# A fused attention and MLP kernel whose matrix products move to halves of TensorE's rows

## The chip, the core and the metric

The kernel runs on one core of a Trainium2 chip. Five engines take part, each with its own instruction queue: TensorE (PE) multiplies matrices, VectorE (DVE), ScalarE (ACT) and GpSimd (POOL) work on elements, and SyncE (SP) issues the transfers (DMA). A product on TensorE has a stationary operand, which a weight load (PEld) puts into the array, and a moving operand, whose columns stream past it. The contraction runs over the rows of the array, which are the 128 partitions of the on-chip memory. Products are summed up in PSUM, which has eight banks. The metric is the device time in microseconds (us), the median of several runs.

## The reference

The input x has 2048 rows of 640. It is normalized, goes through an attention with 32 heads of 20 and a sliding window of 256, and through an MLP of width 1536; the MLP's output gates the attention's.

```
xn = _layernorm(x, axis=-1)
qkv = (xn @ wqkv).reshape(B, S, 3, H, Dh)          # H = 32, Dh = 20
scores = einsum("bhqd,bhkd->bhqk", q, k) * Dh**-0.5
scores = where((i - j >= 0) & (i - j < 256), scores, -1e9)
o = einsum("bhqk,bhkd->bhqd", softmax(scores), v)
s = o.reshape(B, S, D) @ wo
r = maximum(xn @ w1 + b1, 0)
g = silu((r * r) @ w2 + b2)
return x + s * g
```

## The kernel before

The work has three stretches. The first normalizes and transposes x, makes all of V and the first group of Q and K. The middle runs the attention over 16 pairs of heads and 16 tiles of 128 queries, in `steps` = 16·16 + 12 steps, and fills the time on TensorE between its products with the dense products that are left: 32 groups of 15 products for Q and K (tile `qkps`, 512 columns), 48 groups of 15 for the MLP's first matrix (`hps`, 512 columns) and 64 groups of 18 for its second (`yps`, 320 columns). The last stretch multiplies by `wo` (`wops`) and gates.

A dense product is made of three fp32r products (a 4-byte type): each operand is split into a high part and a rest, and high·high, high·rest and rest·high are summed. Q and K for the scores are split into three bf16 parts each. Six pairs of parts lie one under the other, 6·20 = 120 rows (`KR`), so that one product sums them up. The parts are written to memory (`qk_stores`) and read back per pair of heads (`pair_loads`) into `qs` and `ks`.

One step of the middle does, in this order: two score products `sps` of the two heads (`scores`, L448), two products `stps` of the transposed scores of an earlier tile (`scores_t`, L492), the row maxima on DVE (`maxima`, L460), every fourth step the transposition of the maxima (L474) and their copy `mrow` (L478), exponentials on ACT (L499), masking on POOL (L500, L502), a share of the filler (`fill`), the split of the exponentials into two fp16 parts `ph` (ACT, L507) and `pl` (DVE, L513), evacuations of finished dense groups (`flush`), the rest of the filler, and every second step the products with V of two tiles (`values`, L527, 61 columns each, 24 in a full job of two tiles and two heads). What a dense group leaves in PSUM is taken out by `evac`: for Q and K two ACT copies (L780, L784), a DVE subtraction (L781) and a POOL subtraction (L785).

The order of all five queues is written out by hand (`manual_schedule`): what the code emits first stands first. `fill` draws as many products from the generator `filler` as its running total of `cost` allows. PSUM has three banks for dense groups (`pmm`), two for `sps`, two for `stps` and one for the products with V (`po`).

## Time and profile before

| what | us |
|---|---|
| runs | 916.62, 915.09, 917.11 (median 916.62) |
| span of the profiled execution, first to last instruction | 913.8 |
| PE busy | 893.6 (98%) |
| DVE busy | 759.1 (83%) |
| ACT busy | 668.6 (73%) |
| POOL busy | 544.9 (60%) |

The profiled execution's own time outside the span is not listed; its span is 2.8 us under the median of the runs. Matmuls are pipelined and their ends are modelled in the trace, so a busy share of 98% on PE does not yet say that no more would fit. The chain of work that ended last lists, in order of time, what the end of the program hung on; its stretches of like products give the time from one product to the next.

### The profile page before, as it was taken

The numbers are of one execution on the slowest core, as the hardware profiler recorded it, in microseconds if no ns is written. First come the engines' busy times: TensorE is split into PE (matmuls) and PEld (weight loads), VectorE is DVE, ScalarE is ACT, GpSimd is POOL, SyncE is SP. The second block draws the span as 40 slices with busy tenths as digits, with TensorE's granted clock in tenths as the row PEclk, the third lists the DMA queues.
The fourth block names the chain that finished last, engine by engine and source line by source line (L and its number), as shares of the span: only waits on it lengthen the run. The fifth ranks groups of instructions, "written<-read, shape, count | busy, mean of one in ns | idle before, by whom it ended". The sixth has DMA issues, their size and how long they took to land.

```text
span 913.8 us, 21792 instructions
## 1 busy us (share of the span) xinstructions
PE 893.6 (98%) x7632; PEld 746.9 (82%) x7632; DVE 759.1 (83%) x2031; ACT 668.6 (73%) x1282; POOL 544.9 (60%) x832
## 2 busy tenths in 40 slices
PE   8999999999999999999999999999999999999998
PEld 8999977776766678788788788778788788789998
DVE  7875478999899998998888999998988988975554
ACT  5454348898889896987886988976986977994321
POOL 6010017797789785886785876775775976772000
PEclk9999999999999999999999999999999999999999
DMA  6899786767777454244264245365174264156873
GB/s 240 279 394 350 219 266 201 233 209 237 250 237 237 142 180 131 89 155 132 67 203 152 69 123 153 103 224 152 51 262 136 75 211 145 27 158 222 286 272 117
DMA packets 130803, 168.79 MB, mean 185 GB/s; under 512 B 44100, under 2 KB 91268, under 8 KB 128132
## 3 DMA queue, kind: packets, MB, share of 16 engines
q1 hardware_dynamic: 130692, 167.39, 56.3%
q8 instruction: 60, 0.98, 0.4%
q14 instruction: 51, 0.42, 0.1%
HBM read 96.15 MB, written 70.91 MB: 183 GB/s over the span
## 4 chain that ended last, share of the span: by engine, by line
PE 73%; DVE 9%; ACT 8%; DMA 4%; issue 3%; POOL 2%; SPq 1%; ACTq 0%; DVEq 0%; POOLq 0%
PE yps L872 14%; PE hps L578 14%; PE wops L578 8%; PE sps L448 7%; PE qkps L578 7%; PE ops L527 7%; PE stps L492 6%; PE vps L230 5%; ACT p L499 3%; DVE junk L460 2%; PE qkps L200 2%; DVE pl L513 2%; ACT ph L507 1%; DMA v_d<-vt 1%; ACT relu L827 1%
## 5 line engine op out<-in xcount | busy, mean ns | idle before, releaser
L499 ACT ACTIVATE p<-stps,ebias 128x384 f32<-128x384 f32 (+2 forms) x512 | 258.7, 558 | 85.2 <-PE stps L492 72.9
L460 DVE CUSTOM_DVE_ANT_0 junk<-sps,mask 128x384 bf16<-128x384 f32 (+2 forms) x512 | 250.5, 525 | 47.3 <-PE sps L448 40.8
L513 DVE TENSOR_TENSOR pl<-p,ph 128x768 f16<-128x768 f32 (+2 forms) x256 | 251.3, 982 | 1.9 <-ACT ph L507 1.9
L500 POOL TENSOR_SCALAR_AFFINE_SELECT p<-p 128x256 f32<-128x256 f32 x256 | 166.9, 652 | 128.4 <-ACT p L499 112.0
L507 ACT ACTIVATE ph<-p 128x768 f16<-128x768 f32 (+2 forms) x256 | 204.6, 799 | 4.1 <-POOL p L502 3.0
L872 PE MATMUL yps<-w,hh 128*128 128x320 f32 x768 | 183.8, 320 | 0.0
L578 PE MATMUL hps<-xb,w 128*128 128x512 f32 x630 | 172.1, 410 | 0.0
L578 PEld LDWEIGHTS hps<-xb,w 128*128 128x128 f32 x630 | 115.3, 188 | 24.1
L872 PEld LDWEIGHTS yps<-w,hh 128*128 128x128 f32 x768 | 130.7, 188 | 5.0 <-issue 0.6
L448 PE MATMUL sps<-ks,qs 120*128 120x384 bf16 (+2 forms) x512 | 128.2, 319 | 4.5 <-DVE mt L460 4.4
L872 PE MATMUL yps<-w,hl 128*128 128x320 f32 x384 | 122.5, 319 | 0.0
L492 PE MATMUL stps<-qs,ks 122*128 122x384 bf16 (+2 forms) x512 | 120.8, 316 | 1.2 <-DMA qs<-mrow 1.0
L502 POOL TENSOR_SCALAR_AFFINE_SELECT p<-p 128x256 f32<-128x256 f32 x224 | 109.0, 487 | 0.0
L527 PEld LDWEIGHTS <-ph 128*128 128x128 f16 x1440 | 85.9, 97 | 25.6 <-issue 20.6
L527 PE MATMUL ops<-vp,ph 128*128 128x61 bf16 x1440 | 100.9, 192 | 0.0
L527 PE MATMUL ops<-vp,pl 128*128 128x61 bf16 x1440 | 99.7, 191 | 0.0
L831 POOL TENSOR_TENSOR hl<-sq,hh 128x256 fp32r<-128x256 f32 x96 | 77.5, 808 | 18.9 <-DVE sq L830 15.6
L527 PEld LDWEIGHTS <-pl 128*128 128x128 f16 x1440 | 87.7, 97 | 0.0
L872 PEld LDWEIGHTS yps<-w,hl 128*128 128x128 f32 x384 | 72.2, 188 | 1.5
L492 PEld LDWEIGHTS <-ks 122*128 122x128 bf16 x512 | 49.0, 98 | 29.5 <-issue 2.5
L230 PE MATMUL vps<-wv,xT 128*128 128x320 f32 x480 | 71.7, 308 | 0.2 <-DVE r L255 0.2
L230 PEld LDWEIGHTS vps<-wv,xT 128*128 128x128 f32 x480 | 70.5, 188 | 0.6 <-DVE r L255 0.5
(116 smaller groups left out, 1480.3 us busy)
## 6 DMA issues: line engine op xcount, KB each, us to landing
ks<-k_d SPq DMA_DIRECT2D x64, 240.0 KB
qs<-q_d SPq DMA_DIRECT2D x64, 240.0 KB
xb<-xs SPq DMA_DIRECT2D x12, 1280.0 KB
xs<-xT SPq DMA_DIRECT2D x8, 1280.0 KB
y<-ysb SPq DMA_DIRECT2D x32, 320.0 KB
q_d<-shm SPq DMA_DIRECT2D x38, 256.0 KB
v_d<-vt SPq DMA_DIRECT2D x8, 976.0 KB
vp<-v_d SPq DMA_DIRECT2D x16, 488.0 KB
```

Of the source, the lines that this page charges most:

```text
L230: nc.tensor.matmul(ps, xT[xp][b][:, c * BT + t * P: c * BT + (t + 1) * P], wv[wp][:, c, nh * HALF:(nh + 1) * HALF], start=first and m == 0 ...
L448: nc.tensor.matmul(ps[:, :nk], qs[i][0:KR, hh, q * P:(q + 1) * P], ks[i][0:KR, hh, k0 * P:k0 * P + nk], start=True, stop=True)
L460: nc.vector.tensor_tensor_reduce(out=junk[:, :nk], in0=r[hh][:, :nk], in1=mask[:, 3 * P - nk:], scale=1.0, scalar=-3.0e38, op0=ALU.add, op ...
L492: nc.tensor.matmul(ps[:, :n], ks[i][0:KR + 2, hh, kb * P:(kb + 1) * P], qs[i][0:KR + 2, hh, kb * P:kb * P + n], start=True, stop=True)
L499: nc.scalar.activation(p32[:, hh, :n], r[hh][:, :n], AF.Exp, scale=SCALE, bias=ebias)
L500: nc.gpsimd.affine_select(p32[:, :, 0:P], p32[:, :, 0:P], pattern=[[0, 2], [1, P]], compare_op=ALU.is_ge, fill=0.0, base=0, channel_multip ...
L502: nc.gpsimd.affine_select(p32[:, :, 2 * P:], p32[:, :, 2 * P:], pattern=[[0, 2], [-1, P]], compare_op=ALU.is_gt, fill=0.0, base=0, channel ...
L507: nc.scalar.activation(ph[:, :, :n], p32[:, :, :n], AF.Copy)
L513: nc.vector.tensor_sub(pl[:, :, :n], p32[:, :, :n], ph[:, :, :n])
L527: nc.tensor.matmul(ot[:, q % 4, hh, :], t[:, hh, (q - k) * P:(q - k + 1) * P], vp[:, k // 4, k % 4, hh, :], start=m == 1, stop=m == 2 * le ...
L578: nc.tensor.matmul(ps, a, b_, start=j == 0, stop=j == n - 1)
L872: nc.tensor.matmul(pss[nh], hs[fc][hp][:, tt * P:(tt + 1) * P], lin1(wt2, (wp * NFH + fc) * D + nh * HALF, HALF), start=fc == 0 and j == 0 ...
```

## The change

**Halves.** In the middle every product is emitted for 64 of TensorE's 128 rows (`HP`). A dense product and a product with V become two: the first share sums over partitions 0 to 63, the second over 64 to 127, into the same PSUM bank. The scores of the two heads become a product each on its own half: Q and K are now split into two fp32r parts, three pairs of parts make 60 rows (`KR`), head 0 lies at partitions 0 to 59 and head 1 at 64 to 123. The transposition of the maxima is done in two halves, too, into two banks, and copied with two DVE copies.

**Two lanes.** `clock` holds a planned time for each half. `ahead` emits a first share, and before it as many second shares as the other lane's planned time allows (`behind`). Second shares of a dense group wait in `backlog` until all its first shares are emitted; those of the products with V wait in `urgent`, which goes first. Both open `SETTLE` = 0.45 us (planned time) after the last first share. `both` emits a pair of scores. `drain` emits what is left of a queue without first shares in between: after the first part of the filler of each step, and before new products with V. So first shares of one dense group alternate with second shares of the one before.

**Hand-over.** Both shares write one bank, so a group's second share waits for its last first share (`wait_for`, a wait of TensorE on its own semaphore): once for each of the 144 dense groups and each of the 128 jobs of products with V, and products with V wait once more for the job before if they share its bank. A dense group holds its bank from its first share to the end of its evacuation (`Acc`); if all three are held, evacuations are emitted early. Over the whole order that is the case 24 times. Of the 2,880 second shares of products with V, 2,033 are emitted by `drain`.

**Beside it.** The evacuation of Q and K is one ACT copy and one DVE subtraction (the same in the first stretch); the POOL subtraction and the second copy go. Q and K parts are stored as 3 parts of 4 bytes in place of 6 of 2 bytes, with 2 transfers for a group in place of 4 or 3, and read back as 60 rows of 4 KB in place of 120 of 2 KB. The last stretch stays on full rows.

```
-NPART = 6
+NPART = 3
 KR = NPART * DH
+HP = P // 2
...
+COST = {61: 0.0285, P: 0.067, 2 * P: 0.12, HALF: 0.147, 3 * P: 0.172, BT: 0.23}
...
+SETTLE = 0.45
...
-        n = lo.shape[-1]
-        if w == "q":
-            return [(dst[:, 0:2, :], hm), (dst[:, 2, :], lo), (dst[:, 3:5, :], hm), (dst[:, 5, :], hm[:, 0, :])]
-        rep = [hm[:, a, :].unsqueeze(1).to_broadcast([P, 3 - a, n]) for a in range(2)]
-        return [(dst[:, 0:3, :], rep[0]), (dst[:, 3:5, :], rep[1]), (dst[:, 5, :], lo)]
+        twice, once = (slice(0, 3, 2), 1) if w == "q" else (slice(0, 2), 2)
+        return [(dst[:, twice, :], f32(hi).unsqueeze(1).to_broadcast([P, 2, hi.shape[-1]])), (dst[:, once, :], f32(lo))]
...
-                r.append((st[p % 2][0:KR, h, cols], qk_d[w][src, :, cols].rearrange("d a n -> (d a) n")))
+                r.append((f32(st[p % 2])[h * HP:h * HP + KR, cols], qk_d[w][src, :, cols].rearrange("d a n -> (d a) n")))
...
+    def put(j, emit, cost):
+        clock[2] = max(clock[j], clock[2])
+        clock[j] = clock[2] + cost
+        emit()
...
+    def open_for(queue):
+        return queue and queue[0].after is not None and max(clock[1:]) >= queue[0].after + SETTLE
...
+    def behind(queue):
+        job = queue[0]
+        put(1, *job.items.popleft())
...
+    def ahead(emit, cost):
+        while clock[1] <= clock[0]:
+            queue = urgent if open_for(urgent) else backlog
+            if not open_for(queue):
+                clock[1] = clock[0] + 1e-6
+                break
+            behind(queue)
+        put(0, emit, cost)
+
+    def drain(queue, jobs=99):
+        end = max(0, len(queue) - jobs)
+        while len(queue) > end:
+            assert queue[0].after is not None
+            behind(queue)
+
+    def both(first, second, cost):
+        ahead(first, cost)
+        put(1, second, cost)
+
+    def wait_for(made):
+        nop = nc.tensor.nop()
+        tc.add_manual_dep(nop.ins, made.ins.name, HANDOVER, reason="the other half has left the bank")
+
+    def half(j, out, a, b_, **kw):
+        r = slice(j * HP, (j + 1) * HP)
+        return nc.tensor.matmul(out, a[r], b_[r], skip_group_check=True, **kw)
...
-            nc.tensor.matmul(ps[:, :nk], qs[i][0:KR, hh, q * P:(q + 1) * P], ks[i][0:KR, hh, k0 * P:k0 * P + nk], start=True, stop=True)
...
+            o = slice(hh * HP, hh * HP + KR)
+            nc.tensor.matmul(r[hh][:, :nk], qs[i][o, q * P:(q + 1) * P], ks[i][o, k0 * P:k0 * P + nk], start=True, stop=True)
+        both(lambda: one(0), lambda: one(1), COST[nk])
...
-        nc.tensor.transpose(tp, mp, identb)
...
+            nc.tensor.transpose(tps[j], mp[r, :], identb[r, r])
+        both(lambda: one(0), lambda: one(1), COST[61])
...
-            nc.vector.tensor_copy(mrow, tp[0:16, :])
...
+            for j in range(2):
+                nc.vector.tensor_copy(mrow[:, j * HP:(j + 1) * HP], tps[j][0:16, :])
...
-            nc.tensor.matmul(ps[:, :n], ks[i][0:KR + 2, hh, kb * P:(kb + 1) * P], qs[i][0:KR + 2, hh, kb * P:kb * P + n], start=True, stop=True)
...
+            o = slice(hh * HP, hh * HP + KR + 2)
+            nc.tensor.matmul(r[hh][:, :n], ks[i][o, kb * P:(kb + 1) * P], qs[i][o, kb * P:kb * P + n], start=True, stop=True)
+        both(lambda: one(0), lambda: one(1), COST[n])
...
+        drain(urgent)
+        job = Job(lambda: q % 4 == 3 and summed.append((p, q // 4)))
...
+        else:
+            wait_for(passed[0])
...
-                for t in pts[p, k]:
-                    m += 1
-                    nc.tensor.matmul(ot[:, q % 4, hh, :], t[:, hh, (q - k) * P:(q - k + 1) * P], vp[:, k // 4, k % 4, hh, :], start=m == 1, stop=m == 2 * len(ksr))
...
+            def front(ops=ops, m=m):
+                job.mark = half(0, *ops, start=m == 0 and q % 4 == 1, stop=False)
+
+            def back(ops=ops, m=m, ends=k == t and w == 1):
+                if m == 0:
+                    wait_for(job.mark)
+                passed[0] = half(1, *ops, start=False, stop=ends)
+            ahead(front, COST[61])
+            job.items.append((back, COST[61]))
...
+    class Acc:
+
+        def __init__(self, n, name):
+            while not banks:
+                if pending or late:
+                    flush()
+                else:
+                    drain(backlog, 1)
+            self.bank, self.n = banks.pop(0), n
+            self.tile = pmm.tile([P, n], F32, tag=f"mm{self.bank}", name=name)
+
+        def free(self):
+            banks.append(self.bank)
...
+    def halves(job, ps, a, b_, first, last):
+        cost = COST[ps.n]
+
+        def front():
+            job.mark = half(0, ps.tile, a, b_, start=first, stop=False)
+
+        def back():
+            if first:
+                wait_for(job.mark)
+            half(1, ps.tile, a, b_, start=False, stop=last)
+        ahead(front, cost)
+        job.items.append((back, cost))
+        if last:
+            job.after = clock[0]
...
-                    hm = stg.tile([P, 2, BT], BF16, tag="stg", name="shm")
-                    lo = stg.tile([P, BT], BF16, tag="stg", name="slo")
-                    r1 = stg.tile([P, BT], F32, tag="stg", name="srt")
-                    nc.scalar.activation(hm[:, 0, :], ps, AF.Copy)
-                    nc.vector.tensor_sub(r1, ps, hm[:, 0, :])
-
-                    def last():
-                        nc.scalar.activation(hm[:, 1, :], r1, AF.Copy)
-                        nc.gpsimd.tensor_sub(lo, r1, hm[:, 1, :])
-                        posts.extend(qk_stores(w, slice(g * P, (g + 1) * P), slice(b * BT, (b + 1) * BT), hm, lo))
-                    late.append(last)
-                pending.append(evac)
+                    hi = stg.tile([P, BT], F32R, tag="stg", name="shm")
+                    lo = stg.tile([P, BT], F32R, tag="stg", name="slo")
+                    split(hi, lo, ps.tile)
+                    ps.free()
+                    posts.extend(qk_stores(w, slice(g * P, (g + 1) * P), slice(b * BT, (b + 1) * BT), hi, lo))
...
-                    for j, (hp, wp) in enumerate(((0, 0), (0, 1), (1, 0))):
-                        nc.tensor.matmul(pss[nh], hs[fc][hp][:, tt * P:(tt + 1) * P], lin1(wt2, (wp * NFH + fc) * D + nh * HALF, HALF), start=fc == 0 and j == 0, stop=fc == NFH - 1 and j == 2)
...
+                    for hp, wp in ((0, 0), (0, 1), (1, 0)):
+                        jb[2] += 1
+                        halves(job, ps, hs[fc][hp][:, tt * P:(tt + 1) * P], lin1(wt2, (wp * NFH + fc) * D + nh * HALF, HALF), jb[2] == 1, jb[2] == 3 * NFH)
...
-                sc, rows = scores(p, q, between)
-            elif between:
-                rows = between()
+                sc = scores(p, q)
             if b:
                 stp = scores_t(*b)
+            if between:
+                rows = between(sc[0] if a else None)
...
+            drain(urgent)
+            if summed:
+                norm.append(normed(*summed.popleft()))
```

The order on TensorE before, at the end of a job of products with V (`ops`) and the start of a step (the numbers tell the tiles of one name apart):

```order
L527 LDWEIGHTS pl_3286
L527 MATMUL ops_3339<-vp_1_1885,pl_3286 128x61
L448 LDWEIGHTS qs0_120
L448 MATMUL sps_3370<-ks0_121,qs0_120 128x384
L448 LDWEIGHTS qs0_120
L448 MATMUL sps_3372<-ks0_121,qs0_120 128x384
L492 LDWEIGHTS ks0_121
L492 MATMUL stps_3374<-qs0_120,ks0_121 128x384
L492 LDWEIGHTS ks0_121
L492 MATMUL stps_3376<-qs0_120,ks0_121 128x384
L578 MATMUL qkps_3336<-xT0_0_175,wgql_4_3182 128x512
```

Four full-row products for the scores stand in a row, each with a weight load of its own; a dense group (`qkps_3336`) goes on alone. The order on TensorE now, at the start of a step (fp32r products carry their weight load themselves):

```order
L479 MATMUL qkps_2713<-xT0_2_730,wgql_2_1655 128x512
L479 MATMUL qkps_2854<-xT0_2_730,wgkl_2_1723 128x512
L491 MATMUL sps_3000<-ks1_1476,qs1_1475 128x384
L491 MATMUL sps_3001<-ks1_1476,qs1_1475 128x384
L540 MATMUL stps_3004<-qs1_1475,ks1_1476 128x384
L540 MATMUL stps_3005<-qs1_1475,ks1_1476 128x384
L479 MATMUL qkps_3022<-xT0_3_1023,wgqh_2_1653 128x512
L479 MATMUL qkps_3022<-xT1_3_1024,wgqh_2_1653 128x512
L479 MATMUL qkps_2854<-xT0_2_730,wgkh_2_1721 128x512
L479 MATMUL qkps_3022<-xT0_3_1023,wgql_2_1655 128x512
L479 MATMUL qkps_2854<-xT1_2_731,wgkh_2_1721 128x512
```

The two products of a pair of scores follow each other on different halves, and behind them the first shares of `qkps_3022` take turns with the second shares of `qkps_2854`. Now the end of a `drain`, also on TensorE:

```order
L479 LDWEIGHTS ph_2704
L479 MATMUL ops_2761<-vp_0_1488,ph_2704 128x61
L479 LDWEIGHTS pl_2746
L479 MATMUL ops_2761<-vp_0_1488,pl_2746 128x61
L479 LDWEIGHTS ph_2752
L479 MATMUL ops_2761<-vp_0_1488,ph_2752 128x61
L479 LDWEIGHTS pl_2841
L479 MATMUL ops_2761<-vp_0_1488,pl_2841 128x61
L479 MATMUL qkps_2854<-xT0_2_730,wgkh_2_1721 128x512
L479 MATMUL qkps_2713<-xT1_2_731,wgqh_2_1653 128x512
L479 MATMUL qkps_2854<-xT1_2_731,wgkh_2_1721 128x512
L479 MATMUL qkps_2713<-xT0_2_730,wgql_2_1655 128x512
```

Twenty-four second shares of products with V stand in a row there (the last four are shown), with no first share among them; before, such a job was 24 full-row products and stood, as the fence of before shows, right ahead of the scores. DVE at the start of a step with a copy of the maxima, before:

```order
L460 ISA junk_3669,mt_3668<-sps_3659,mask_94 128x128
L460 ISA mt_3668 128x1
L460 ISA junk_3671,mt_3668<-sps_3662,mask_94 128x128
L460 ISA mt_3668 128x1
L478 COPY mrow_3673<-sps_3659 16x128
L538 RECIPROCAL rs_3675<-osb_3654 128x8
L513 TENSOR_TENSOR pl_3689<-p32_3575,ph_3623 128x768
L781 TENSOR_TENSOR srt_3693<-qkps_3544,shm_3691 128x512
```

And now:

```order
L501 ISA junk_4295,mt_4294<-sps_4284,mask_94 128x128
L501 ISA mt_4294 128x1
L501 ISA junk_4297,mt_4294<-sps_4285,mask_94 128x128
L501 ISA mt_4294 128x1
L524 CAST mrow_4299<-sps_4284 16x64
L524 CAST mrow_4299<-sps_4285 16x64
L561 TENSOR_TENSOR pl_4339<-p32_4175,ph_4244 128x768
L111 TENSOR_TENSOR slo_4342<-qkps_3994,shm_4341 128x512
```

One copy of 128 columns has become two of 64, and the subtraction of the Q and K evacuation (`slo`) stands where the one of before (`srt`) stood, with nothing on ACT and POOL after it.

More of the change, by code (lines that the diff above doesn't have):

```diff
@@ L1 @@
+from collections import deque
 from contextlib import ExitStack
@@ L579, in mm_group, with open_job, done, mm_halves @@
             yield cost
+    banks = [0, 1, 2]
+    class Acc:
[20 more added lines that the diff above has]
+        if last:
+            job.after = clock[0]
+    def open_job(evac, *then):
+        def done():
+            pending.append(evac)
+            for f in then:
+                f()
+        job = Job(done)
+        backlog.append(job)
+        return job
+    def mm_halves(ps, mms, work, evac, *then):
+        job = open_job(evac, *then)
+        for j, (a, b_) in enumerate(mms):
+            halves(job, ps, a, b_, j == 0, j == len(mms) - 1)
+            yield work
     def lin(tiles, off, n):
@@ L861, in filler @@
[L861 to L877 removed]
+                place = [None]
@@ new lines, in filler, with start, evac @@
+                jobs = []
+                def start(nh, hf=hf, t=t, place=place, idx=4 * (n - NB) + tt, end=n == NB - 1 and tt == 3, n=n, tt=tt):
+                    sl = slice(nh * HALF, (nh + 1) * HALF)
+                    ps = Acc(HALF, "yps")
+                    def evac():
+                        vload[0] += 0.5
+                        if not nh:
+                            place[0] = wgt.tile([P, D], F32, tag="wgqh", name="ysb")
+                        ysb = place[0]
+                        nc.vector.tensor_add(ysb[:, sl], ps.tile, (yins[t] if hf else b2t)[:, sl])
+                        ps.free()
@@ L884, in filler @@
                     load(1)
-            if n == NB - 1:
-                shut.discard("21")
+            if n < last and nxt:
+                xb, its = nxt
+            else:
+                its = []
+        drain(backlog)
+        flush()
+        flush()
         ensure("o")
```

258 lines of the change are left out of this document (132 added, 126 removed).

## The prediction

> **What bounds the kernel now.** First the page's head: the span, the busy shares, and the chain that ended last.
>
> ```profile
> span 913.8 us, 21792 instructions
> PE 893.6 (98%) x7632; PEld 746.9 (82%) x7632; DVE 759.1 (83%) x2031; ACT 668.6 (73%) x1282; POOL 544.9 (60%) x832
> PE 73%; DVE 9%; ACT 8%; DMA 4%; issue 3%; POOL 2%; SPq 1%; ACTq 0%; DVEq 0%; POOLq 0%
> ```
>
> The chain is PE for 73%. The change is in the middle, so I read the busy time of each engine for that stretch, and for the hundred microseconds in which DVE is busiest.
>
> ```profile
> core 0: us, PE busy (x) PEld busy (x) DVE busy (x) ACT busy (x) POOL busy (x), PEclk, DMA share, GB/s
> 118.50:825.00 706.50, 693.95 (x6247) 553.34 (x6246) 634.05 (x1761) 590.28 (x1122) 521.86 (x796) 1.00 0.51 162
> 500.00:600.00 100.00, 98.62 (x911) 78.32 (x911) 95.53 (x261) 90.47 (x175) 76.90 (x119) 1.00 0.39 119
> ```
>
> DVE stands close behind PE: 634.05 of 706.5 us. To see whether PE is truly full there, I take the time from one product to the next from unbroken stretches of the chain (columns: start, length, engine, tile, line, count).
>
> ```profile
> 13.28 5.56 PE qkps L200 x45
> ...
> 72.62 2.18 PE tps L167 x20
> ...
> 407.07 0.70 PE ops L527 x24
> ...
> 407.94 0.06 PE sps L474
> ...
> 408.49 2.05 PE yps L872 x14
> 410.54 0.34 PE sps L448 x2
> 410.88 0.33 PE stps L492 x2
> ...
> 450.77 2.06 PE hps L578 x9
> ```
>
> That is 0.146 us for a dense product of 320 columns (2.05/14), 0.229 for 512 (2.06/9), 0.170 and 0.165 for a score product, 0.029 for one with V (0.70/24), 0.06 for a transposition of maxima, 0.124 for 256 columns of fp32r (5.56/45) and 0.109 for an fp32 transposition of 128 columns. The counts:
>
> ```profile
> L872 PE MATMUL yps<-w,hh 128*128 128x320 f32 x768 | 183.8, 320 | 0.0
> L872 PE MATMUL yps<-w,hl 128*128 128x320 f32 x384 | 122.5, 319 | 0.0
> L448 PE MATMUL sps<-ks,qs 120*128 120x384 bf16 (+2 forms) x512 | 128.2, 319 | 4.5 <-DVE mt L460 4.4
> L492 PE MATMUL stps<-qs,ks 122*128 122x384 bf16 (+2 forms) x512 | 120.8, 316 | 1.2 <-DMA qs<-mrow 1.0
> L527 PE MATMUL ops<-vp,ph 128*128 128x61 bf16 x1440 | 100.9, 192 | 0.0
> L527 PE MATMUL ops<-vp,pl 128*128 128x61 bf16 x1440 | 99.7, 191 | 0.0
> L474 PE MATMUL sps<-identb,mp 128*128 128x128 bf16 x63 | 14.0, 222 | 6.2 <-DVE mp L465 6.0
> ```
>
> 1,152 products of 320 columns are 168.7 us; 80 groups of 15 (32 `qkps`, 48 `hps`, by the loops) of 512 are 274.7; of the 1,024 scores 896 have 384 columns and make 150.1, and the 128 narrow ones, taken at 0.12 and 0.06, 11.5; 2,880 with V are 84.0; 64 transpositions 3.8. The sum is 692.8 of 706.5 us, so 13.7 us of the stretch are not PE's work. PE bounds the middle, and every microsecond of its work counts.
>
> **The change, part by part.**
>
> *Scores.* Two heads on two halves at once cost one product's time. For fp32r with 384 columns there is no row; between the rows of 320 and 512 columns lies 0.174 (0.146 + a third of 0.083). 448 pairs are 78.0 us, 32 pairs of 256 columns at 0.124 are 4.0, and 32 of 128 at 0.109 at most are 3.5: 85 in place of 161.6. This is the gain, 76 us. Its bounds are nothing gained (the halves take turns) and half of today's time, 81.
>
> *Dense products.* The number doubles to 4,704 shares. If two shares run side by side, a pair costs what the full-row product costs now: 443.4 us, no change. Whether they do, no row shows, since nothing ran on part of the rows. The bounds are 0 and +443.4 (each share alone). A point between depends on weight loads. The rows on loads:
>
> ```profile
> 404.93 0.11 PEld L448 LDWEIGHTS <-qs 120*128 120x128 bf16 x2
> L872 PEld LDWEIGHTS yps<-w,hh 128*128 128x128 f32 x768 | 130.7, 188 | 5.0 <-issue 0.6
> ```
>
> Two 2-byte loads, which take 98 ns each, fit into 0.11 us, so they start some 12 ns apart. A 4-byte load takes 188 ns, and with the transpositions above a product with one never follows faster than 0.109 us. If the loads of both halves use one path at that spacing, a pair of shares costs at least 0.218: nothing for 512 columns, +0.072 for 320 and +0.044 for a pair of scores. I take the loads as parallel for the forecast, because the loads of today already run under the product before (188 ns of load within a spacing of 0.146), and price the other case as a rival. The Trainium skill speaks against it: "TensorE: Matmul & The Clock Gate", section "LDWEIGHTS (loading the stationary operand)", says that the time of a load goes by its columns, not by its rows, 128/1.2 GHz = 107 ns. The 0.109 above agrees; a load of half the rows is in no trace here. By that rule, with one load at a time, the sum is the first rival's. The same skill, "TensorEngine Tiling (Array Packing)", section "Key Properties", says that different tiles can load and multiply in parallel; by it the sum is the forecast's, and no row here shows it.
>
> *Products with V.* 2,880 pairs of shares side by side would stay at 84.0. But 2,033 second shares are emitted by `drain` with no first share among them: 58 us (0.0285 each) on one half alone. The one dense first share ahead of each of the 128 drains runs beside them, some 0.15 us each, 19 us. So 39 us are lost; bounds 0 (first shares slip beside them) and 84 (none is ever covered).
>
> *Transpositions of maxima.* 64 pairs of half the width, 2 us in place of 3.8.
>
> PE's sum is 443.4 + 85 + 84 + 39 + 2 = 653, and with the 13.7 us that are not PE's today, 667.
>
> *Hand-overs.* 272 waits of PE on itself, and behind each stands everything else in PE's queue. They come 0.45 us of planned work after the share they wait for, and the longest product ends 0.41 us after its start (the busy 410 ns of the 512-column rows below). So most are met; I take 0.01 us on average, 3 us, with bounds 0 and 0.1 us each, 27.
>
> ```profile
> L578 PE MATMUL hps<-xb,w 128*128 128x512 f32 x630 | 172.1, 410 | 0.0
> L877 DVE TENSOR_TENSOR ysb<-yps,yin 128x320 f32<-128x320 f32 x32 | 15.3, 479 | 2.4 <-DMA yin<-y 2.4
> ```
>
> *Banks.* 24 times all three banks are held, and PE's next first share waits for an evacuation just emitted: 0.48 us on DVE (L877) behind up to 1.0 us of another DVE instruction. Bounds 0 and 24·1.5 = 36; I take 0.25 each, 6, since the emission runs ahead of the engine. PE's line is then 676.
>
> *DVE.* It loses no work: the `srt` subtraction becomes `slo`, one for one. It gains 64 copies: two of 64 columns for one of 128.
>
> ```profile
> L478 DVE COPY mrow<-sps 16x128 bf16<-16x128 bf16 x63 | 13.1, 207 | 0.0
> L538 DVE RECIPROCAL rs<-osb 128x8 f32<-128x8 f32 x64 | 11.7, 183 | 4.6 <-ACT osb L534 4.5
> L460 DVE CUSTOM_DVE_ANT_0 junk<-sps,mask 128x384 bf16<-128x384 f32 (+2 forms) x512 | 250.5, 525 | 47.3 <-PE sps L448 40.8 <-PE sps L474 4.7
> L785 POOL TENSOR_TENSOR slo<-srt,shm 128x512 bf16<-128x512 f32 x32 | 41.8, 1305 | 31.3 <-ACT shm L784 30.4 <-POOL slo L785 0.6
> L784 ACT ACTIVATE shm<-srt 128x512 bf16<-128x512 f32 x32 | 20.3, 634 | 4.7 <-DVE srt L781 4.7
> ```
>
> Even a row of 8 elements takes 183 ns, so a short copy is some 0.18: +11 us, 645 in all. The best hundred microseconds ran DVE at 95.5%; at that share 645 us of work need 675. 40.8 us of DVE's idle time now are waits for `sps`, which come sooner; what is late next is the evacuation and `pl`, on which the products with V wait.
>
> *ACT, POOL, transfers.* ACT loses 20.3 us and POOL 41.8 in the middle; both were off the chain or short there, so I count nothing. Transfers move the same bytes in fewer, longer pieces, with some 70 fewer issues on SP; the DMA share is 0.51 in the middle and covers it. The first stretch gives up one ACT copy and one DVE subtraction per group under PE's work, nothing either. The last stretch is as before.
>
> PE's line (676) and DVE's (675) are as good as equal, and two engines that wait for each other at the same length lose a little more: I take 680. That is 26.5 us less than 706.5: a span of 887.3, and with the 2.8 us by which the median lies over the profiled span, **890**. If nothing of these extras falls due, the middle is 653 and the time 863; if hand-overs and banks cost their upper bounds (27 + 36 on 667), 730 and 940.
>
> **The rivals.**
>
> 1. *The weight loads of the halves take turns* (the other side). Place: dense products of 320 columns and score pairs. 1,152·0.218 = 251.1; 512·0.218 = 111.6; 512-column pairs 274.7; V 84 + 39, transpositions 2: 762, with 13.7 of other work 776. If loads spread perfectly under the longer products, the load path alone holds 5,728·0.109 + 5,760·0.012 = 693 us, with other work 707. So 0 to +70 us, about +44: 960. It decides from 0.088 us per 4-byte load, where 3,328 loads of the pairs of 320 and of scores bring the sum back to 706.5. For it speaks that no row has a 4-byte load closer than 0.109; against it, that a transposition may be slow for another reason.
> 2. *Shares of different lengths do not run side by side,* only equal ones. Then both shares of the products with V stand alone, 168 in place of 84 + 39: 698 + 13.7 = 712, +5, with hand-overs and banks +14: 931. In the extreme no two shares overlap, the change then doesn't do what it says: 443.4·2 + 168 + 162 + 4 + 14 = 1,235, +528, some 1,445.
> 3. *DVE takes the bound and keeps today's share.* 634 of 706.5 is 89.7%; 645 at that share is 719, +12.5: 929. Halfway to the forecast, at 92.5%, it is 697: 907. It decides at 91.3%, where 645 us fill 706.5. For it speak the in-order queues and banks held longer; against it, the 40.8 us of waits for `sps` and the 95.5%.
>
> **How the numbers follow.** Forecast (863 to 908): 0.48. First rival (916 to 987): 0.24. Second: 0.09, and 0.04 for its extreme. Third (908 to 930): 0.15, half of it ahead of 916.6. A difference within 0.2% (1.8 us) is about what a measurement of this kernel can't tell from none. Faster takes the forecast and 0.08 of the third and second, same 0.04 of rivals one to three, slower the rest: 0.56, 0.04, 0.40. For 8 in 10 the range reaches from 866 to 965: nearly all of the forecast, the third rival, most of the second and over half of the first. The likeliest case alone is 866 to 908.
>
> **What would show it.** Side by side: in the chain or by starts, two `sps` of a step start together and the next dense share 0.17 us later, and pairs of `yps` shares go at 0.146 us a pair; PE's busy count doubles while the middle ends some 26 us sooner. Rival one: pairs of 320 columns at 0.22, those of 512 still at 0.23. Rival two: `ops` shares that start only where the dense share ends. Rival three: DVE's waits move from `sps` to evacuations, PE waits for DVE (`mt`, `ysb`) and its chain share falls under 73%. Hand-overs: PE idle behind its own semaphore more than 3 us in all. The forecast is wrong if a 320-column pair takes over 0.176 us (0.088 twice), or if DVE in the middle stays under 91%.

## The result: 14.6% slower

| | us |
|---|---|
| before, median of 4 runs | 915.86 (913.65 to 917.11) |
| after, median of 4 runs | 1048.67 (1047.81 to 1050.35) |
| ratio after/before, 95% interval | 1.1459 (1.1437 to 1.1482) |
| forecast | 890 (866 to 965) |

The forecast has the wrong sign, and the time lies 84 us above its range. The page of the changed kernel, its head and the chain that ended last:

```profile
span 1046.6 us, 32696 instructions
PE 935.6 (89%) x12928; PEld 870.1 (83%) x12928; DVE 755.6 (72%) x2085; ACT 652.0 (62%) x1240; POOL 506.9 (48%) x800
PE 67%; DVE 17%; ACT 6%; issue 5%; POOL 2%; DMA 2%; SPq 0%; DVEq 0%; POOLq 0%; ACTq 0%
```

PE's share fell from 98% to 89%, DVE's from 83% to 72%, and DVE's part of the chain rose from 9% to 17%. No engine is full any more. The stretches say where. First the busy time per stretch of the changed kernel, then of the kernel before (the same columns). The second stretch ends with the last `yps` product, at 959.6 and 828.1 us:

```profile
core 0: us, PE busy (x) PEld busy (x) DVE busy (x) ACT busy (x) POOL busy (x), PEclk, DMA share, GB/s
118.50:290.00 171.50, 170.74 (x2524) 156.66 (x2524) 157.14 (x463) 133.84 (x240) 101.16 (x153) 1.00 0.79 247
290.00:960.00 670.00, 567.42 (x9044) 522.03 (x9041) 481.29 (x1370) 445.92 (x854) 384.94 (x613) 0.93 0.38 111
```

```profile
118.50:290.00 171.50, 165.52 (x1305) 121.57 (x1303) 154.98 (x420) 140.91 (x255) 129.79 (x174) 1.00 0.75 236
290.00:828.00 538.00, 531.44 (x4984) 434.66 (x4983) 479.70 (x1343) 449.78 (x869) 393.35 (x624) 1.00 0.44 140
```

The loss is all in the second stretch, where the MLP's groups are the filler: 670 us in place of 538. PE is idle there for 102.6 us (670 less 567.42) in place of 6.6, and the granted clock fell from 1.00 to 0.93. In the first stretch PE is full. One group of rows of the last products for Q and K, after and then before, by the starts of the first and the last:

```profile
L479 PE MATMUL qkps<-xT,wgkl x160: 383/390/502, 122.8 to 288.4; 64*128 64x512 f32 x160
```

```profile
L578 PE MATMUL qkps<-xT,wgkl x80: 387/389/537, 121.9 to 292.4; 128*128 128x512 f32 x80
```

That took 165.6 us in place of 170.5, although the changed kernel also started products of the MLP in it, the first at 282.8 us. So the changed kernel won 3% or a little more as long as Q and K were the filler.

What PE waited for in the second stretch of the changed kernel (columns: sum in us, times, longest):

```profile
PE yps L479 <- DVE ysb L970: 36.0, 30, 2.2
PE yps L479 <- DVE sq L940: 28.1, 18, 3.0
PE hps L479 <- DVE sq L940: 14.8, 16, 2.0
PE yps L479 <- ACT hh L938: 8.6, 8, 1.4
PE hps L479 <- DVE ysb L970: 8.6, 8, 1.9
PE yps L479 <- POOL hl L941: 5.3, 8, 1.2
```

These six rows are 101.4 of the 102.6 us. Four of them, 87.5 us in 72 waits, are waits for an evacuation: `ysb` takes a `yps` group out of its bank, `sq` an `hps` group. The kernel before has no such row in this stretch. The other two, 13.9 us, are waits for the MLP's hidden values (`hh` and `hl`), which are made from `sq`. One such wait, in the chain of the changed kernel:

```profile
445.14 0.10 PE sps L491
...
445.27 0.56 DVE junk L501
...
445.83 0.47 DVE junk L501
...
446.71 0.41 DVE ysb L970
...
447.17 1.62 PE yps L479 x19
```

PE has issued a pair of scores and comes to a share of `yps`, for which no bank is free. The evacuation that would free one stands in DVE's queue behind the maxima of the scores just made. PE stands still for 1.66 us, and everything behind that share stands with it, the next scores too. That starves DVE in turn: its waits for `sps` at the maxima rose from 32.9 to 102.0 us. The two engines run by turns. The stop shown is no exception: of the 102.6 us in which PE stands still, the trace has DVE at work on `pl` for 32.2, on the maxima for 16.0 and on `sq` and `ysb` themselves for 36.3.

### The profile page after: what moved, and what is told of

Its sections match the earlier page's. It is cut to its first block, busy times and chain, and to the rows that moved or that the text cites. A ratio compares the mean times of both kernels' runs of the same rounds, so it can differ in the third digit from the quotient of the medians.

```text
span 1046.6 us, 32696 instructions
## 1 busy us (share of the span) xinstructions
PE 935.6 (89%) x12928; PEld 870.1 (83%) x12928; DVE 755.6 (72%) x2085; ACT 652.0 (62%) x1240; POOL 506.9 (48%) x800
## 4 chain that ended last, share of the span: by engine, by line
PE 67%; DVE 17%; ACT 6%; issue 5%; POOL 2%; DMA 2%; SPq 0%; DVEq 0%; POOLq 0%; ACTq 0%
PE yps L479 13%; PE ops L479 10%; PE qkps L479 10%; PE hps L479 9%; PE vps L230 7%; PE wops L641 7%; DVE pl L561 5%; DVE junk L501 5%; PE sps L491 4%; PE stps L540 3%; ACT p L547 3%; PE qkps L207 2%; DVE sq L940 2%; DVE ysb L970 2%; DMA y<-ysb 1%
## 5 line engine op out<-in xcount | busy, mean ns | idle before, releaser
L479 PE MATMUL yps<-w,hh 64*128 64x320 f32 x1536 | 284.5, 338 | 73.1 <-DVE ysb L970 36.0
L479 PEld LDWEIGHTS yps<-w,hh 64*128 64x128 f32 x1536 | 213.9, 201 | 89.7 <-DVE ysb L970 45.2
L479 PE MATMUL hps<-xb,w 64*128 64x512 f32 x1260 | 246.6, 413 | 20.8 <-DVE sq L940 12.2
L479 PE MATMUL ops<-vp,ph 64*128 64x61 bf16 x2880 | 213.4, 193 | 0.1
L479 PE MATMUL ops<-vp,pl 64*128 64x61 bf16 x2880 | 210.5, 192 | 0.0
L479 PE MATMUL yps<-w,hl 64*128 64x320 f32 x768 | 204.2, 334 | 5.3 <-POOL hl L941 5.3
L479 PEld LDWEIGHTS hps<-xb,w 64*128 64x128 f32 x1260 | 168.4, 190 | 30.4 <-DVE ysb L970 10.6
L479 PEld LDWEIGHTS <-ph 64*128 64x128 f16 x2880 | 182.3, 96 | 12.6 <-issue 7.7
L479 PEld LDWEIGHTS <-pl 64*128 64x128 f16 x2880 | 185.8, 97 | 0.0
L479 PEld LDWEIGHTS yps<-w,hl 64*128 64x128 f32 x768 | 132.4, 201 | 7.6 <-POOL hl L941 7.6
```

Source lines behind the costliest of these rows:

```text
L479: return nc.tensor.matmul(out, a[r], b_[r], skip_group_check=True, **kw)
```

## The experiments

### Do halves run side by side, and what does a change to them cost?

**Scores alone on halves.** Dense products, products with V and the transposition stay on full rows in the order of before, but for the transposition of the maxima, which comes behind all four score products; Q and K are split and stored as in the changed kernel.

```
+            o = slice(hh * HP, hh * HP + KR)
+            nc.tensor.matmul(r[hh][:, :nk], qs[i][o, q * P:(q + 1) * P], ks[i][o, k0 * P:k0 * P + nk], start=True, stop=True)
```

> Only the scores run on halves (60 fp32r rows for each head, the two-part split of Q and K, their evacuations and transfers); dense products, products with V and the transposition of the maxima stay on full rows, in the order of the kernel before. Bank theory (the changed kernel loses its time because a dense group holds its PSUM bank for twice as long): banks are held as before here, so the gain of the scores shows, PE's sum in the middle is 443 + 85 + 84 + 4 + 14 = 630 us, DVE's 645 at 95.5% bound it at 675: about 885 us in all. Rival (halves as such are slow, or a change between half and full rows costs a drain): two changes in each of 267 steps at 0.15 to 0.3 us each put 80 to 160 us on the 630: 920 to 1000 us.

Measured: 929.75, ratio 1.0179 (1.0163 to 1.0195). Products on PE in the order of time (start, length, x count), then their weight loads, in the trace of this kernel:

```profile
404.85 0.31 PE L849 MATMUL yps<-w,hh 128*128 128x320 f32 x1
405.08 0.45 PE L433 MATMUL sps<-ks,qs 60*128 60x384 f32 x2
405.37 0.34 PE L476 MATMUL stps<-qs,ks 62*128 62x384 f32 x2
405.64 0.42 PE L849 MATMUL yps<-w,hh 128*128 128x320 f32 x1
405.89 0.31 PE L849 MATMUL yps<-w,hl 128*128 128x320 f32 x1
```

```profile
405.08 0.19 PEld L433 LDWEIGHTS sps<-ks,qs 60*128 60x128 f32 x2 [0.19 <-issue]
405.19 0.19 PEld L476 LDWEIGHTS stps<-qs,ks 62*128 62x128 f32 x2
405.64 0.19 PEld L849 LDWEIGHTS yps<-w,hh 128*128 128x128 f32 x1 [0.26 <-issue]
```

The two products of a pair start together (3 ns apart by the starts behind the row x2), and two 4-byte loads fit into 0.19 us, the time of one. So halves run side by side, and their loads do not take turns. But from 404.85 to 405.89 it is 1.04 us, while two dense products at 0.146 and two pairs at 0.174 make 0.64. The visit to half rows costs 0.40 us; in 256 steps that is 102 us, more than the 76 that the pairs save. The excess of 26 us is somewhat more than the 16 measured. The loads show the place: the first load on halves starts 0.19 us and the next one on full rows 0.26 us after the load before it has ended, while the loads of a run of dense products follow each other without a gap. PE stayed full at a clock of 1.00.

**The two pairs of a step apart.** To see whether it is the change between full and half rows that costs, or each pair, the transposed pair of this kernel is moved behind the first part of the filler: two visits in a step in place of one, the same pairs. The same move in the kernel before is the control.

```
-            if b:
-                stp = scores_t(*b)
...
+            fill(EARLY_FILL * per)
             if b:
+                stp = scores_t(*b)
                 exs[b] = (exps(*b, *stp), stp[1])
-            fill(EARLY_FILL * per)
```

> The kernel with the scores alone on halves, with the transposed pair of each step moved behind the early part of the filler, so that the two pairs of a step no longer stand next to each other. In the kernel with the pairs next to each other the trace shows three joints in a step: a full-row product of 512 columns to the first pair 0.318 us from start to start (0.231 between two of them), the pair to the transposed pair 0.278 (0.174 for 384 columns), the transposed pair to a full-row product 0.267. Theory A (every pair whose two halves start together shows its weight load once, about 0.09 us at its start, and about as much at the next full-row product): one joint more in 256 steps, 20 to 30 us over the kernel with the pairs together, 945 to 960 us, less what the move of the kernel before itself costs, which is run beside it. Theory B (it is the change between half and full rows that costs, and a pair behind a pair costs nothing): two changes more in each step at 0.14 us, 65 to 80 us more, 990 to 1010 us. Theory C (TensorE has room, the joints hide): within 10 us of the kernel with the pairs together.

> The kernel before, on full rows, with the transposed score products moved behind the early part of the filler in the same way: the control for the kernel with half-row pairs apart. If the move itself is harmless: 910 to 925 us. If the later start of the exponentials costs: 930 us or more; that difference is then taken off the other kernel's.

Measured: 1024.92, ratio 1.1213 (1.1184 to 1.1242); the control 926.23, ratio 1.0133 (1.011 to 1.0156). The move alone costs 12 us. What is left of 95.2 us over the kernel with the pairs together is 83 us, 0.32 for each visit more. PE in the trace with the pairs apart:

```profile
404.81 1.66 PE L562 MATMUL hps<-xb,w 128*128 128x512 f32 x6
406.39 0.45 PE L433 MATMUL sps<-ks,qs 60*128 60x384 f32 x2
406.77 0.74 PE L562 MATMUL hps<-xb,w 128*128 128x512 f32 x2
407.44 0.44 PE L476 MATMUL stps<-qs,ks 62*128 62x384 f32 x2
407.80 0.50 PE L562 MATMUL hps<-xb,w 128*128 128x512 f32 x1
```

From 404.81 to 407.80 it is 2.99 us; eight dense products at 0.229 and two pairs at 0.174 make 2.18. That is 0.40 us for each of two visits, with one pair in each, as it was for one visit with two pairs; over the whole run a visit more is 0.32. So the price belongs to the change and not to the pair (theory B, which gave too little: the runs came out 15 us above its 1010, about the 12 us of the move). The Trainium skill has the rule: "TensorEngine Tiling (Array Packing)", section "Key Properties", says that a change of the tiling mode drains TensorE. The traces agree that the change costs, and give it a price, 0.40 us in and out; whether a drain of the array makes it, or the weight load that doesn't run ahead there, no run tells apart. The changed kernel, whose middle is on halves throughout, does not pay it; one that is on halves only for its scores does.

### Is it the banks?

A dense group on full rows fills its bank in one go. On halves it has its first shares beside the second shares of the group before, and then its second shares beside the first shares of the next. Two of the three banks are always being filled, and one group's time in place of two is left for an evacuation. The theory: this is what PE waits for. The rival: PE's own work, or the products with V, make the time.

**No products with V, three banks and four.** Both kernels leave out the products with V and normalize a constant in their place. That frees a bank, which one of the two gives to the dense groups.

```
+        nc.scalar.activation(osb, b2t[:, 0:8 * VW].rearrange("p (a w) -> p a w", w=VW), AF.Copy)
...
-    banks = [0, 1, 2]
+    banks = [0, 1, 2, 3]
```

> The changed kernel without the products with V (the normalisation reads a constant tile in their place, so the output is not the reference's): 84 us of first and second shares, the drains and their hand-overs are gone. Bank theory: the dense groups still have three banks and still wait for evacuations; PE's sum would allow a middle of 560 and DVE's a middle of 675, but it stays above 740: about 950 to 1000 us. Rival (the drains and the hand-overs of the products with V are the loss): the middle falls to DVE's 675 or so: about 890 us.

> The same without the products with V, and the PSUM bank that these held given to the dense groups: four banks in place of three. Bank theory: the waits of TensorE for evacuations (DVE sq, DVE ysb) nearly go, the clock stays full, and DVE's work bounds the middle at 675 to 690: about 890 to 905 us, 60 us or more under the run with three banks. Rival (banks are not what PE waits for): the same time as with three banks, within 1%.

Measured: 1089.2 with three banks, ratio 1.192 (1.1895 to 1.1945), and 912.25 with four, 0.9985 (0.9973 to 0.9997). With three banks that is 89 us above the range that the theory gave, with four 7 us. With less work on PE and three banks the kernel is slower than the changed one: the groups follow each other faster, and each evacuation has, it seems, still less time. PE's waits with three banks, then the largest with four, both between 290 and 960 us (the MLP's last product starts at 1002.9 and 825.1 us):

```profile
PE hps L479 <- DVE sq L919: 61.4, 24, 3.5
PE yps L479 <- DVE ysb L949: 45.7, 35, 2.5
PE yps L479 <- DVE sq L919: 40.2, 18, 4.3
PE hps L479 <- DVE ysb L949: 28.8, 19, 2.2
```

```profile
PE yps L479 <- ACT hh L917: 15.1, 13, 2.6
PE yps L479 <- POOL hl L920: 12.7, 17, 1.9
...
PE yps L479 <- DVE sq L919: 2.9, 4, 1.2
PE yps L479 <- DVE ysb L949: 2.6, 5, 0.8
```

The waits for evacuations fall from 176.1 us to 7.3 (the two rows shown and 1.8 at `hps`), and the time by 177. One bank is worth a sixth of the time. The waits for `hh` and `hl` do not fall with them; they are 27.8 us here. The kernel with four banks says one thing more, in the window of the middle that the prediction used:

```profile
118.50:825.00 706.50, 646.32 (x5846) 560.41 (x5845) 628.89 (x1825) 573.21 (x1091) 501.71 (x768) 0.96 0.54 164
```

DVE is busy for 628.89 of 706.5 us, 89.0%, and PE is idle for 60. So even with the products with V gone and a bank more, the middle is no shorter (the last `yps` product starts at 825.1 us, in the kernel before at 828.1), and DVE does not get to the share that the forecast needs.

**The kernel before with two dense banks.** Full rows, the old order, one bank less.

```
-    pmm = ctx.enter_context(tc.tile_pool(name="pmm", bufs=3, space=PSUM))
+    pmm = ctx.enter_context(tc.tile_pool(name="pmm", bufs=2, space=PSUM))
```

> The kernel before, full rows throughout, with two PSUM banks for dense groups in place of three. Then an evacuation has the time of one group (15 times 0.229 us, or 18 times 0.147) until its bank is wanted, as in the changed kernel with three banks, where two are always being filled. Bank theory: TensorE waits for DVE sq and DVE ysb here too and the clock drops at times: 960 to 1050 us. Rival (the waits belong to the halves and their order): 913 to 925 us.

Measured: 960.41, ratio 1.0495 (1.0465 to 1.0526), at the lower end of what the theory gave. The waits of the changed kernel come up in it, `yps` for `ysb` with 13.7 us and for `sq` with 8.3, `hps` for `sq` with 9.4. The granted clock was 0.99 in the stretch of the MLP, so hardly any of this is the clock. By the count of banks alone, two on full rows should cost as much as three on halves; why they are milder, no run shows.

### Would earlier evacuations do?

**Three flushes in a step.** The changed kernel; finished groups are evacuated at three places of a step in place of one.

```
+            flush()
             post_all()
...
             fill((1 - EARLY_FILL) * per + SWING * (-1) ** (s - LAG - 3))
+            flush()
```

> The changed kernel, with evacuations emitted at three places of a step in place of one, so that each stands up to a step earlier in the queues of ACT and DVE. Bank theory: TensorE's waits for evacuations (some 120 us between 290 and 960 us of the changed kernel) shrink, and with them the stretches at half clock: 960 to 1010 us. Rival (the shares or the clock are slow by themselves): no change, 1045 to 1050 us.

**At once.** As above, but an evacuation is emitted where the group's last share is, and that of `hps` in one piece.

```
-            pending.append(evac)
+            evac()
```

> The changed kernel with each dense group's evacuation emitted as soon as its last second share is emitted, the evacuation of hps in one piece, and evacuations of what is left at three places of a step. Bank theory: a bank is held for the shortest time that the queues allow, so TensorE waits less for DVE than in the run with three places alone (970 us): 930 to 960 us. Rival (the length of the hold is settled by ACT's and DVE's queues, not by when the evacuation is emitted; an evacuation that stands too early blocks the maxima and exponentials behind it): 965 us or more.

Measured: 970.54, ratio 1.0628 (1.0589 to 1.0667), and 978.31, ratio 1.0691 (1.0665 to 1.0716). The banks are the same, and the place of the evacuations alone takes 78 us off the changed kernel. With three flushes the waits of `yps` for `ysb` and `sq` are down, from 64.1 us in the changed kernel:

```profile
PE yps L479 <- DVE ysb L970: 10.8, 13, 2.5
PE yps L479 <- DVE sq L940: 8.8, 9, 2.2
```

With the row of `hps` they are 19.9 us, and yet the kernel is 57 us over the one before, so waits for evacuations are not all of the loss. (The 120 us that the expectations give for them in the changed kernel are too many; PE's four rows are 87.5.) Emitting still earlier gains nothing: an evacuation that stands in the queue before its group is done holds up DVE. Its waits of `sq` for the first step on ACT rose from 11.2 us in the changed kernel to 22.7 and 51.5, those of `ysb` for the group itself from 3.3 to 7.6 and 10.1.

### A fourth bank with all the work

**Four dense banks.** PSUM has no bank left, so the four score products of a step share three banks in place of two and two, and the transposed pair stands behind the first part of the filler.

```
-    pat = ctx.enter_context(tc.tile_pool(name="pat", bufs=2, space=PSUM))
+    pat = ctx.enter_context(tc.tile_pool(name="pat", bufs=3, space=PSUM))
...
-        r = [pat.tile([P, 3 * P], F32, tag="st", name="stps") for _ in range(2)]
+        r = [pat.tile([P, 3 * P], F32, tag="s", name="stps") for _ in range(2)]
...
-    banks = [0, 1, 2]
+    banks = [0, 1, 2, 3]
```

> The changed kernel, complete, with four banks for dense groups. The fourth comes from the scores, which share three banks in place of two and two; to make that fit, the pair of transposed scores stands after the first part of the filler in place of right behind the pair of scores. Evacuations are emitted as in the changed kernel. Bank theory: TensorE's waits for evacuations fall from some 120 us to under 40 and the half clock nearly goes: 915 to 960 us. Rival (products with V, drains and hand-overs lose the time): 1000 us or more, since all of these stay.

> Four banks as in the run before this one, and evacuations emitted at three places of a step. Bank theory: both remedies together leave PE's line at 653 + 12 (pairs of 320 columns take 0.157, not 0.146) + 14 and DVE's at 675 to 700 of middle: 890 to 925 us. Rival (the two engines' in-order queues keep DVE at some 90% of the middle whatever the banks): 925 us or more.

Measured: 1065.88, ratio 1.1646 (1.1618 to 1.1675), and with the early flushes 1118.8, ratio 1.2228 (1.2195 to 1.2262). Both miss what the theory had given. The rival's times came, but not its cause: no wait on products with V stands among PE's. Between 290 and 960 us the first of them waits most for this (PE, then its weight loads):

```profile
PE stps L540 <- DVE mrow L524: 18.4, 35, 1.1
PE stps L540 <- DVE mt L501: 17.7, 21, 2.0
```

```profile
PEld stps L540 <- DVE mt L501: 47.2, 115, 2.2
```

The waits for `ysb` and `sq` are gone, as the fourth bank should have it. The same kind of wait has come up at the banks of the scores, now for the maxima and their copies (36.1 us in the two PE rows; with the early flushes, up to 1020 us, 71.9). It holds in the first stretch too, where the last Q and K product starts at 324.3 us in place of 288.4.

**The move alone.** Is it the later place of the transposed scores that cost this, or the banks that they share? The changed kernel with three dense banks and two and two for the scores, with only the move.

> The changed kernel with three dense banks and two plus two banks for scores, as it was; the two transposed score products of a step only stand behind the early part of the filler, as they do in the two kernels with four dense banks. Theory (in the four-bank kernel it is the three banks that all four score products share which cost what the fourth dense bank gave): without sharing the move alone changes little, 1030 to 1065 us, the waits of yps for ysb stay near the changed kernel's 36 + 45 us, and waits of the transposed scores for the masks mt on VectorE stay under 15 us. Rival (the later place of the transposed scores is what cost it, since the exponentials start later): 1080 us or more, with waits of the transposed scores for mt of 30 us or more.

Measured: 1053.63, ratio 1.15 (1.1474 to 1.1525), 5 us over the changed kernel. No transposed product waits for the maxima; the four evacuation rows are there again with 62.0 us, `ysb` at `yps` with 20.6 of the 36 expected:

```profile
PE yps L479 <- DVE sq L940: 27.0, 18, 2.9
PE yps L479 <- DVE ysb L970: 20.6, 17, 3.1
```

So it was the shared banks: the dense groups' gain was lost again at the scores. Taking the bank from another user with all the work in place was not run.

## Why the prediction was wrong, step by step

- **Banks: the step that failed.** The prediction counted the 24 places in the order at which all three banks are held when a first share is emitted, 0.25 us each, 6 us with a bound of 36. Measured: 72 waits of 1.2 us on average, 87.5 us, more than twice the bound. The 24 are only those at which the emission found no free bank. An evacuation that is emitted in time but stands in DVE's queue behind maxima and `pl` of the step holds its bank as well; so at least 48 of the 72 waits are at places that were not counted. The term should have been worked out from the time of a bank: filled for two groups' times in place of one, with DVE's queue of one step as the latency of an evacuation. The kernels with three and four banks without V, 177 us apart, and the kernel before with two show it.
- **The hidden values, not in the sum.** Waits for `hh` and `hl` are 13.9 us. The banks are not their cause: with four banks they are 15.8 us with all the work and 27.8 without V.
- **The clock, not in the sum.** The second stretch ran at 0.93. The clock that the traces record is full or half and nothing between; 0.93 of 670 us is then some 94 us at half (0.07·2·670; the record itself has 89, in 15 pieces). Eighteen shares of `yps` took 2.77 us at half clock (0.50 granted) and 1.53 a little later (0.88 granted, since the first 0.36 us of it were still at half):

```profile
505.48 2.77 PE yps L479 x18
...
508.89 1.53 PE yps L479 x18
```

  So at most half of the 94 us is lost, 47; the starts below make it 33. The Trainium skill, "TensorE: Matmul & The Clock Gate", section "A second HAM failure mode: psum-queue depth-cycling", describes a like case: a kernel that cycles through PSUM banks idles so often in short pieces between its groups of products that the clock gate swings between half and full. The trace agrees: where the waits are largest, without V on three banks, the same stretch had 0.88; with three flushes a step it had 0.98. But with four banks and no V, where few waits for evacuations are left and PE still stands idle for 60 us, it was 0.96 over the middle.
- **Dense products: right, or a little low.** Shares run side by side near the price forecast. PE in an undisturbed piece behind a wait of the changed kernel, then a longer stretch of its chain:

```profile
695.51 0.31 PE L479 MATMUL yps<-w,hl 64*128 64x320 f32 x2
695.66 0.46 PE L479 MATMUL yps<-w,hh 64*128 64x320 f32 x4
695.96 0.31 PE L479 MATMUL yps<-w,hl 64*128 64x320 f32 x2
```

```profile
443.60 1.55 PE yps L479 x19
```

  Six shares in 0.45 us are 0.15 a pair, 0.146 forecast; nineteen in 1.55 are 0.163. Pairs of 512 columns stand 0.23 us apart by the starts in the trace, 0.229 forecast.
- **Scores: right in a run of equal shares, more beside others.** Two heads together take one product's time. In the stretch of Q and K, in the chain of the changed kernel:

```profile
227.79 0.18 PE sps L491 x2
227.97 0.18 PE stps L540 x2
...
229.43 0.19 PE ops L479 x6
...
229.79 0.33 PE sps L491 x2
```

  A pair is 0.18, 0.174 forecast; right behind products with V it can be 0.33. Over the middle, at full clock, it is 0.205 on average.
- **Products with V: the sum about right, the reason not.** No two of them stand side by side: `values` drains a job's second shares before the next job's first ones, so they follow each other on one half. There their shares start some 0.03 us apart (0.19/6), first and second ones alike, so 5,760 of them take about 164 us at 0.0285 in place of 84 + 39. But a dense share between two of them costs only some 0.02 more; by the starts in the trace 658 of the 4,704 dense shares lie so. At 0.073 to 0.115 us for a share elsewhere that gives back some 35 to 60.
- **Hand-overs: right.** PE's waits for itself are 0.2 us in that list; its weight loads wait for it for 15.2, the most (6.1) from `hps` to `hps`, but beside running products.
- **DVE: the 95.5% over the whole middle came in no run.** In the middle it came to 76%, starved by PE's stops, which is under the 91% that the prediction had named as a sign of being wrong. Without V and with four banks it was 89.0%. The third rival's share, 89.7%, was the better guess, and two of its signs came (PE waits for `ysb`, its chain share under 73%), but DVE's waits for `sps` grew in place of going, and DVE was not the bound.
- **The other rivals.** Loads that take turns: false (two in 0.19 us). A load of half the rows takes 184 ns (median of `yps`), one of all rows 188. The 0.109 us that the prediction took as a sign of one load at a time is the spacing of transpositions; the loads in its own rows are 188 ns with 4 bytes and 98 with 2. Unequal lengths that do not overlap: false, since a dense share runs beside products with V.

The 132.0 us between the two middles (841.5 and 709.5) come out so: PE idle, 103.3 in place of 12.6, is 90.7; PE's busy time, 738.2 in place of 697.0, is 41.3. The forecast had 653 us of work in that busy time, 85 less than the 738. The starts in the trace take these 85 apart, each product counted from its start to the next one's, without PE's idle time. The products that start at half clock take 33 us more than as many of their kind at full clock. The last product before each of PE's 96 stops counts as busy to its own end, though the next one comes only after a pause: 24 us more than its usual share, so the stops cost more than the idle time says. Of the rest, scores take 100 us in place of 85, dense products and products with V together 577 in place of 566, transpositions of maxima 4 in place of 2. The middle is 161 us over the forecast's 680. Some 100 of it are the stops (103.3 and 24, less the 27 that the forecast had beside PE's work), 33 the half clock, 15 the scores. That the clock fell because of the waits is argued from the stretches; no run changed one without the other. In the first stretch, without waits, the gain came near the forecast's 26.5 of 706.5 us (2.9% or a little more, 3.8% forecast).

## What to carry over

Splitting a product over halves of the rows about keeps TensorE's time and doubles the time in which its bank is being filled; before such a change, count for each bank how long it is filled and how long its evacuation can stand in another engine's queue, and not how often the emission finds none free. One share without a bank also delays the products behind it in TensorE's queue, and with them those that feed the engine it waits for, as in the stop of 1.66 us above. And half rows can pay only where a long stretch stays on them: each visit from full rows and back was 0.32 to 0.40 us.

## What was unexpected of the hardware

- Two 4-byte loads for the two halves take 0.19 us together, as long as one.
- A visit to half rows and back cost 0.40 us in the traces, with one pair in it or two, and 0.32 on average over a run.
- Products with V of 61 columns start 0.03 us apart in a row on one half; a dense share of the other half among them costs some 0.02 us more, where a dense share by itself costs 0.073 to 0.115.
- The recorded clock is half or full. With waits of up to 3.0 us in the stretch of the MLP it was 0.93 there on average, and 0.88 where they were more and longer (up to 4.3). Eighteen shares took 2.77 us at 0.50 and 1.53 at 0.88.
